# Routing arithmetic of the first half moved from VectorE to GpSimd, with PSUM banks marked as taken

## The chip, the cores and the metric

One core of a Trainium2 chip runs the whole program. The metric is the device time of one execution, in microseconds (us). Five engines work side by side, each through its own queue in order: TensorE (PE, weight loads shown as PEld), VectorE (DVE), ScalarE (ACT), GpSimd (POOL) and SyncE (SP, which here only starts DMAs). Data move between engines through SBUF and through PSUM, the eight accumulator banks that TensorE writes.

## The reference

```python
# attention, q k v: (4, 8, 1152, 64)
q_pool = q.reshape(B, H, S // 2, 2, D).mean(axis=3)
scores = scale * np.matmul(q_pool, k.transpose(0, 1, 3, 2))
scores = scores - np.max(scores, axis=-1, keepdims=True)
attn = np.exp(scores);  attn /= np.sum(attn, axis=-1, keepdims=True) + 1e-09
x = (attn @ v) as 2304 tokens x 512
# mixture of 8 experts, the best two of each token
noisy = x @ w_gate + np.log1p(np.exp(x @ w_noise)) * noise
top2_w = softmax of the two largest of noisy
out[token] += top2_w[k] * (np.maximum(x @ w1[e], 0) @ w2[e])   # for both chosen experts
```

## The kernel before, in words

The program has three stages: attention, routing, experts. Values are held as pairs of 16-bit numbers (a high and a low part), so most products are made of three matmuls.

**Attention** works on 16 pairs (a head of two batches), each with three query groups of 384, 48 segments in all. For each step of work `score` writes a chunk of scores to one of two wide PSUM tiles (`pss`), ScalarE takes the exponential into `pf`, and the low part `pl` = `pf` - high(`pf`) is made by `p_lo` on whichever of POOL (two halves of 128x384, L358) and DVE (one piece of 128x768, L355) the planner chooses. Then `pv` multiplies with the values. Ahead of it run the row maxima: `max_mm` and `max_rest` (L297) on TensorE, `max_relu` on ScalarE, `max_red` (L311) and `rest_red` (L320) on DVE. The four single PSUM banks (`psm`) are shared by the maxima, the `pv` sums and the routing.

**What sets the order.** `Plan` is a list scheduler that runs when the program is written: every piece of work has an engine, a cost, a due key and what it waits for, and the planner writes the pieces into the engines' queues in the order in which its own clock starts them. On the chip each queue runs in that order.

**Routing** is `Route.steps`, a generator that gives one piece at each `yield`. It is run four times: once for the first half of the tokens (`j=0`, nine blocks of 128 tokens, so tiles of 128x72), in the second half of attention; and three times for the second half (`j=1`, three blocks each, 128x24), beginning at the end of attention. These three are called groups 0, 1 and 2 here; what of them the planner has not placed when attention ends is written out by `advance`, in steps of `PACE`, between the pieces of `Moe.early`. A run transposes its rows by DMA into `xTg` tiles (L671; three tiles a group, and four buffers for all of them), multiplies by the gate weights (L681, 36 matmuls a group), evicts (L685), computes a softplus by polynomials (L690 to L734), the noisy logits (L737, L739), the two largest (L744, L748), a one-hot mask (L759), the rank of each token in its expert by matmul (L767, L769), a slot number (L792), a small table beside each row (L796 to L799), and then scatters every row twice into the expert lists `xg` in DRAM (L99, 18 indirect DMAs on POOL's queue for each half).

**Experts.** `Moe.early` works on the first 256 rows of the first two experts, which the first half's scatter has filled, while the second half is routed; `mm1` (L937) and `mm2` (L958) are the matmuls, `flush` evicts `mm1` (L946 on ScalarE, L947 on DVE), `split` (L882, L884) makes the weights' two parts. `Moe.run` loads the other rows (`xT<-xg`, L892) only after the last scatter, and then goes through all experts. `Base.bank` hands out the four `psm` banks in rotation.

Of the kernel before, what the change touches and what calls it, by code (L numbers as in the profile page):

```python
# [9 lines left out]
F32 = mybir.dt.float32  # L10
# [9 lines left out]
P = 128  # L20
# [8 lines left out]
E = 8  # L29
# [37 lines left out]
class Base:  # L67
    def __init__(s, tc, ctx):
        s.tc, s.nc = tc, tc.nc
        s.const = ctx.enter_context(tc.tile_pool(name="const", bufs=1))  # L70
        ps = ctx.enter_context(tc.tile_pool(name="ps", bufs=1, space=PSUM))
        s.wides = [ps.tile([P, 2, 512], F32, name=f"pss{x}") for x in range(2)]
        s.banks = [ps.tile([P, 512], F32, name=f"psm{x}") for x in range(4)]
        s.sp = s.const.tile([1, 1], F32, name="sp")
        s.raw = {"kr": s.const.tile([P, 2 * NK, D], F32, name="kr"), "qr": s.const.tile([P, NCQ, 2, D], F32, name="qr"),
                 "vr": s.const.tile([P, 2 * NK, D], F32, name="vr"), "kn": s.const.tile([P, 2 * NK, P], F16, name="kn")}
        s.given = None
        s.nw = s.nb = 0

    def flat(s, name):  # L80
# [130 lines left out]
class Attn:  # L211
# [306 lines left out]
    def others(s, F0, out):  # L518
# [30 lines left out]
    def route(s, gen, key, deps, slack, soft=False, then=None, pace=0.0):  # L549
        G = s.G  # L550
# [6 lines left out]
        def piece(bank, held):  # L557
# [30 lines left out]
class Route:  # L588
# [55 lines left out]

    def steps(s, j, gs, pool, nt, nu, gap):
        nc = s.nc
        V = nc.vector
        C = 3 * len(gs)

# [7 lines left out]
        def U(shape, dt=F32):  # L657
            n = 1
            for x in shape:
                n *= x  # L660
            t = pool.tile([P, C * 2 * E], dt, name=f"ru{C}", bufs=nu)[:, 0:n]
            if len(shape) == 3:
                return t.rearrange("p (c k e) -> p c k e", c=shape[0], k=shape[1])
            return t.rearrange("p (c e) -> p c e", c=shape[0])
        L = U([C, 2 * E])
        for x, g in enumerate(gs):
# [18 lines left out]
            V.tensor_scalar(L[:, 3 * x:3 * x + 3], ps, 1.0 / (XS * GS), None, op0=ALU.mult)  # L685
            yield (0.0, "SP", 1.35) if gap and x + 1 < len(gs) else None
        lg = L[:, :, 0:E]
        t = L[:, :, E:]
        a = T([C, E])
# [5 lines left out]
        V.tensor_scalar(k, a, LOG2E, RND, op0=ALU.mult, op1=ALU.add)  # L695
        yield
        V.tensor_scalar(k, k, RND, None, op0=ALU.subtract)
        yield
        r = T([C, E])
        V.scalar_tensor_tensor(r, k, -LN2H, a, op0=ALU.mult, op1=ALU.add)  # L700
        yield
        V.scalar_tensor_tensor(r, k, -LN2L, r, op0=ALU.mult, op1=ALU.add)
        kb = T([C, E], I32)
        V.tensor_scalar(kb, k, 127.0, 8388608.0, op0=ALU.add, op1=ALU.mult)
        yield
        p = T([C, E])
        V.tensor_scalar(p, r, EXPC[0], None, op0=ALU.mult)
# [5 lines left out]
        V.scalar_tensor_tensor(e, p, 1.0, kb.bitcast(F32), op0=ALU.add, op1=ALU.mult)  # L713
        yield
        z = T([C, E])
        V.tensor_scalar(z, e, 2.0, None, op0=ALU.add)
        yield
        V.reciprocal(z, z)
        yield
        V.tensor_mul(z, z, e)  # L720
        yield
        z2 = T([C, E])
        V.tensor_mul(z2, z, z)
        yield
        V.tensor_scalar(p, z2, LOGC[0], None, op0=ALU.mult)
        rl = T([C, E])
        V.tensor_scalar(rl, t, 0.0, None, op0=ALU.max)
        yield
        for cc in LOGC[1:]:
            V.scalar_tensor_tensor(p, p, cc, z2, op0=ALU.add, op1=ALU.mult)  # L730
            yield
        V.scalar_tensor_tensor(p, p, 1.0, z, op0=ALU.add, op1=ALU.mult)
        yield
        V.scalar_tensor_tensor(p, p, 2.0, rl, op0=ALU.mult, op1=ALU.add)  # L734
        yield
        c0 = j * NCQ + gs[0] * 3
        V.tensor_mul(p, p, s.nz[:, c0:c0 + C])  # L737
        yield
        V.tensor_add(p, p, lg)  # L739
        yield  # L740
        m8 = T([C, E])
        ix = T([C, E], U32)
        for c in range(C):
            V.max(out=m8[:, c], in_=p[:, c])  # L744
            if c % 3 == 2:
                yield
        for c in range(C):
            V.max_index(out=ix[:, c], in_max=m8[:, c], in_values=p[:, c])  # L748
            if c % 3 == 2:
                yield  # L750
        d = T([C, 1])
# [4 lines left out]
        V.tensor_copy(idx, ix[:, :, 0:2])  # L756
        yield
# [4 lines left out]
        V.memset(mk[:, C], 0.0)  # L762
        yield
        V.tensor_add(mk[:, 0:C], oh[:, :, 0], oh[:, :, 1])
        yield (0.1, "PE", 0.6) if gap else WAIT_RK
        pr = s.B.bank()[:, 0:(C + 1) * E].rearrange("p (c e) -> p c e", e=E)
        nc.tensor.matmul(pr.rearrange("p c e -> p (c e)"), s.tri, mk.rearrange("p c e -> p (c e)"), start=True, stop=False)  # L767
        for c in range(C):
# [3 lines left out]
        sm = T([C, 1])  # L772
        V.tensor_scalar(sm, e2, 1.0, 1e-9, op0=ALU.add, op1=ALU.add)
        yield (0.2, "DVE", 0.35) if gap else None
        rk = U([C + 1, E])
        V.tensor_add(rk, pr, s.n0[:, None, :].to_broadcast([P, C + 1, E]))
        V.reciprocal(w[:, :, 0:1], sm)
        yield
        q = U([C, 2, E])
        V.tensor_mul(q, oh, rk[:, 0:C, None, :].to_broadcast([P, C, 2, E]))  # L780
        s.n0 = s.per.tile([P, E], F32, name=f"n{j}{gs[0]}")
        if j == 0:
            V.tensor_max(s.n0, rk[:, C], s.floor)
# [46 lines left out]
class Moe:  # L830
# [89 lines left out]
    def mm1(s, e, f, a=0, b=CAP):  # L920
# [109 lines left out]
def overflow_body(tc, a, R, w1, w2, out):  # L1030
# [26 lines left out]
    with tc.For_i(0, E, 1) as e:  # L1057
# [15 lines left out]
        with tc.For_i(0, nt, 1):  # L1073
# [102 lines left out]
```

## Time and profile before

| | us |
|---|---|
| median of 3 runs | 889.57 (889.2 to 894.68) |
| the profiled execution | 891.44 |
| its span, first to last instruction | 889.6 |
| PE busy | 812.4 (91%) |
| DVE busy | 532.0 (60%) |
| ACT busy | 444.1 (50%) |
| POOL busy | 393.3 (44%) |

Shares over the whole span mix the stages. Attention lasts to about 442 us, the changeover with the second half's routing to about 503 us, and the rest is the experts. A line such as "L355 DVE TENSOR_TENSOR pl<-pf" is an instruction of line 355 on DVE that writes a tile `pl` from `pf`.

### The profile page before, as it was taken

How to read it: one execution, taken by the hardware profiler on the slowest of the kernel's cores; microseconds unless marked ns; L12 is line 12 of the kernel's file. 1: busy time of each engine (PE TensorE's matmuls, PEld its weight loads, DVE VectorE, ACT ScalarE, POOL GpSimd, SP SyncE). 2: the span in 40 equal slices, each digit the busy share in tenths (PEclk: the TensorE clock that was granted, in tenths of full speed). 3: DMA queues.
4: the chain of work that ended last, by engine and by line, in shares of the span. 5: the costliest groups of instructions: out<-in, count | busy, mean ns of one | idle time of the engine just before them, and what ended most of it. 6: DMA issues, size and time to landing. Idle time of an engine off the chain costs nothing. (4 is left out here: it accounts for less than half of the span.)

```text
span 889.6 us, 21173 instructions
## 1 busy us (share of the span) xinstructions
PE 812.4 (91%) x8686; PEld 534.3 (60%) x8686; DVE 532.0 (60%) x1276; ACT 444.1 (50%) x663; POOL 393.3 (44%) x378
## 2 busy tenths in 40 slices
PE   3889999999989778899979799999999999999995
PEld 1547777677767645678756365756474655647542
DVE  4878898899889898899888141334233231422200
ACT  4658878787877466676534132333233232322310
POOL 4448889887984777674307312020202102020222
PEclk9989999999999889999999999999999999999998
DMA  8899796897899469566568836282927456290143
GB/s 195 174 230 246 159 235 177 194 207 182 196 220 190 117 157 227 122 180 142 126 156 299 203 72 141 74 214 71 226 60 202 84 137 148 72 225 14 24 54 43
DMA packets 213639, 137.81 MB, mean 155 GB/s; under 512 B 150305, under 2 KB 183585, under 8 KB 213537
## 3 DMA queue, kind: packets, MB, share of 16 engines
q1 hardware_dynamic: 204896, 116.33, 53.9%
q0 software_dynamic: 8640, 20.08, 11.1%
q8 instruction: 69, 1.13, 0.5%
q14 instruction: 34, 0.27, 0.1%
HBM read 62.14 MB, written 35.44 MB: 110 GB/s over the span
## 5 line engine op out<-in xcount | busy, mean ns | idle before, releaser
L358 POOL TENSOR_TENSOR pl<-pf 128x384 f16<-128x384 f32 x278 | 269.6, 999 | 103.9 <-ACT pf L350 90.9
L350 ACT ACTIVATE pf<-pss 128x768 f32<-128x768 f32 x216 | 173.5, 813 | 62.6 <-PE pss L343 54.3
L99 POOL DMA_INDIRECT out_dram<-y,mti x40 | 62.2, 1556 | 315.8 <-ACT y L963 306.6
L378 PEld LDWEIGHTS <-pf 128*128 128x128 bf16 x2880 | 158.6, 99 | 47.7 <-issue 18.2
L378 PE MATMUL psm<-vv,pf 128*128 128x65 f16 (+1 forms) x2880 | 168.9, 195 | 2.3 <-DVE mx L311 1.2
L378 PE MATMUL psm<-vv,pl 128*128 128x65 f16 (+1 forms) x1440 | 159.9, 194 | 2.7 <-POOL pl L358 1.9
L342 PE MATMUL pss<-qt,kt 128*128 128x384 f16 (+1 forms) x576 | 151.4, 292 | 2.9 <-ACT pf L350 2.9
L343 PE MATMUL pss<-qt,kt 66*128 66x384 f16 (+1 forms) x576 | 151.7, 292 | 0.1
L947 DVE SCALAR_TENSOR_TENSOR hl<-pss,hh 128x640 f16<-128x640 f32 (+2 forms) x68 | 50.2, 738 | 157.3 <-ACT hh L946 157.3
L378 PEld LDWEIGHTS <-pl 128*128 128x128 f16 x1440 | 127.8, 100 | 3.3 <-POOL pl L358 2.2
L958 PE MATMUL psm<-wh,hh 128*128 128x512 f16 x320 | 122.0, 381 | 0.0
L958 PE MATMUL psm<-wl,hh 128*128 128x512 f16 x320 | 122.0, 381 | 0.0
L958 PE MATMUL psm<-wh,hl 128*128 128x512 f16 x320 | 122.0, 381 | 0.0
L311 DVE CUSTOM_DVE_ANT_0 rd<-psm,rd 128x512 f32<-128x512 f32 x144 | 97.4, 684 | 24.3 <-ACT rd L305 20.1
L946 ACT ACTIVATE hh<-pss 128x640 f16<-128x640 f32 (+2 forms) x68 | 43.2, 635 | 131.6 <-PE pss L937 131.6
L958 PEld LDWEIGHTS <-hh 128*128 128x128 f16 x640 | 62.7, 98 | 74.0 <-issue 0.8
L963 ACT ACTIVATE y<-psm,mg 128x512 f32<-128x512 f32 x40 | 27.5, 688 | 153.9 <-issue 82.1
L297 PE MATMUL psm<-kt,qt 128*128 128x512 f16 (+3 forms) x320 | 79.9, 325 | 23.0 <-DVE mx L311 10.4
L305 ACT ACTIVATE rd<-psm 128x512 f32<-128x512 f32 x144 | 86.1, 598 | 22.4 <-PE psm L297 17.4
L937 PE MATMUL pss<-xT,fh 128*128 128x320 f16 (+1 forms) x448 | 84.4, 305 | 5.7 <-DMA xT<-xg 5.7
L355 DVE TENSOR_TENSOR pl<-pf 128x768 f16<-128x768 f32 x77 | 87.1, 1145 | 0.0
L937 PE MATMUL pss<-xT,wh 128*128 128x320 f16 (+1 forms) x448 | 83.4, 303 | 0.0
(158 smaller groups left out, 1134.7 us busy)
## 6 DMA issues: line engine op xcount, KB each, us to landing
xg<-zt SPq DMA_DIRECT2D x40, 260.0 KB
kr<-in_k_dram SPq DMA_DIRECT2D x32, 288.0 KB
vr<-in_v_dram SPq DMA_DIRECT2D x16, 576.0 KB
kr<-in_moe_w_dram SPq DMA_DIRECT2D x17, 512.0 KB
qr<-in_moe_w_dram SPq DMA_DIRECT2D x16, 512.0 KB
kn<-in_moe_w_dram SPq DMA_DIRECT2D x16, 512.0 KB
qr<-in_q_dram SPq DMA_DIRECT2D x31, 256.0 KB
vr<-in_moe_w_dram SPq DMA_DIRECT2D x15, 512.0 KB
```

Of the source, the lines that this page charges most:

```text
L99: i = nc.gpsimd.indirect_dma_start(out=out, out_offset=bass.IndirectOffsetOnAxis(ap=idx, axis=0), in_=src, in_offset=None, **kw)
L297: s.nc.tensor.matmul(ps[r, o:o + m.shape[1] * P], s.G.buf["qt", i][:, c, r], m, start=True, stop=True)
L305: s.nc.scalar.activation(s.G.buf["rd", i, c], s.G.buf["D", i, c], AF.Relu)
L311: s.nc.vector.tensor_tensor_reduce(out=rd, in0=s.G.buf["S", i, c], in1=rd, scale=1.0, scalar=-3.0e38, op0=ALU.add, op1=ALU.max, accum_out= ...
L342: mm(ps[:, a, o:o + w], kt[:, hh * NK + kc, :], qf[:, q0:q0 + w], start=True, stop=False)
L343: mm(ps[:, a, o:o + w], kt2[0:66, hh * NK + kc, :], qf2[0:66, q0:q0 + w], start=False, stop=True)
L350: s.nc.scalar.activation(s.parts(u)[0], s.G.buf["ps", u][:, :, 0:SG], AF.Exp, scale=0.125 / (IN_SCALE * IN_SCALE))
L355: s.nc.vector.tensor_sub(pl, pf, ph)
L358: s.nc.gpsimd.tensor_sub(pl[:, a], pf[:, a], ph[:, a])
L378: mm(o[:, 0:x], src[:, t % 2, ci * P:ci * P + P], vv[:, hh * NK + kc, a:a + x], start=st, stop=last and src is pl, skip_group_check=True)
L937: nc.tensor.matmul(ps[:, i, 0:N], w[:, dc, f * P:(f + 1) * P], xT[:, 2 * dc + x, i * N:(i + 1) * N], start=(n == 0), stop=(n == 11))
L958: nc.tensor.matmul(ps, h[:, f, b * P:(b + 1) * P], w[:, f, :], start=(n == 0), stop=(n == 23))
```

## The change

In the first half's routing (`steps(0, ...)`) the elementwise steps go to POOL. A DVE instruction that does two operations on two tensors (`scalar_tensor_tensor`) becomes two on POOL: a `tensor_scalar` into a scratch tile `tm`, and a `tensor_tensor`; the planner sees two pieces. Reciprocals, MAX8, the index search, the one-hot compare, the reduction and what reads PSUM stay on DVE. The first step takes max(-t, t), so the signs of the steps behind it change. The planner is told that those pieces are POOL's (`home`). Apart from this, `bank` now skips a bank that has been handed out and whose reader has not been written yet. The second half's routing stays on DVE; only one multiplication in it (L789) comes one place later.

```diff
     def bank(s):
+        s.taken = None
         if s.given is not None:
             return s.given
         s.nb += 1
-        return s.banks[s.nb % 4]
+        assert len(s.busy) < 4
+        while s.nb % 4 in s.busy:
+            s.nb += 1
+        s.taken = s.nb % 4
+        s.busy.add(s.taken)
+        return s.banks[s.taken]
...
-        s.route(R.steps(0, (0, 1, 2), s.sm, 14, 6, 0.8), 245, [s.ev[n] for n in range(24)], 3.0, then=then, pace=0.8)
+        s.route(R.steps(0, (0, 1, 2), s.sm, 14, 6, 0.8, "POOL"), 245, [s.ev[n] for n in range(24)], 3.0, then=then, pace=0.8, home="POOL")
...
-            wait, eng, cost = d if isinstance(d, tuple) else (0.0, "DVE", 0.3)
+            wait, eng, cost = d if isinstance(d, tuple) else (0.0, home, 0.3)
...
+        W = V if eng == "DVE" else nc.gpsimd
+        dve = None if eng == "DVE" else (0.1, "DVE", 0.3)
...
+        def stt(o, x, c, y, op0, op1):
+            if W is V:
+                V.scalar_tensor_tensor(o, x, c, y, op0=op0, op1=op1)
+                return
+            W.tensor_scalar(tm, x, c, None, op0=op0)
+            yield
+            W.tensor_tensor(o, tm, y, op=op1)
...
-        V.scalar_tensor_tensor(a, t, -1.0, t, op0=ALU.mult, op1=ALU.min)
-        yield
-        V.tensor_scalar(a, a, -87.0, None, op0=ALU.max)
+        V.scalar_tensor_tensor(a, t, -1.0, t, op0=ALU.mult, op1=ALU.max)
+        yield
+        W.tensor_scalar(a, a, 87.0, None, op0=ALU.min)
...
-            V.scalar_tensor_tensor(p, p, cc, r, op0=ALU.add, op1=ALU.mult)
+            yield from stt(p, p, cc, r, ALU.add, ALU.mult)
...
-            V.tensor_copy(mt[:, :, 0:1], s.tok[:, c0 + 3 * x:c0 + 3 * x + 3, None])
+            W.tensor_copy(mt[:, :, 0:1], s.tok[:, c0 + 3 * x:c0 + 3 * x + 3, None])
...
             s.nc.scalar.activation(hh, ps, AF.Relu)
             s.nc.vector.scalar_tensor_tensor(hl, ps, 0.0, hh, op0=ALU.max, op1=ALU.subtract)
+            s.B.busy.discard(bk)
```

Since the planner's clock runs differently once these pieces stand elsewhere, everything behind them is ordered anew. Three places follow; line numbers of the second of each pair are those of the changed file.

GpSimd's queue from the place where the first half's arithmetic begins, before:

```order
L358 TENSOR_TENSOR pl_114<-pf_113 128x384 x2
L358 TENSOR_TENSOR pl_110<-pf_109 128x384 x2
L358 TENSOR_TENSOR pl_112<-pf_111 128x384 x2
L358 TENSOR_TENSOR pl_114<-pf_113 128x384 x2
L358 TENSOR_TENSOR pl_116<-pf_115 128x384 x2
L358 TENSOR_TENSOR pl_118<-pf_117 128x384 x2
```

and now (`rt` and `ru` are the routing's tiles):

```order
L365 TENSOR_TENSOR pl_114<-pf_113 128x384 x2
L365 TENSOR_TENSOR pl_110<-pf_109 128x384 x2
L712 TENSOR_SCALAR rt_5344<-rt_5344 128x72
L715 TENSOR_SCALAR rt_5361<-rt_5344 128x72
L717 TENSOR_SCALAR rt_5361<-rt_5361 128x72
L679 TENSOR_SCALAR rt_5345<-rt_5361 128x72
L681 TENSOR_TENSOR rt_5385<-rt_5345,rt_5344 128x72
```

Twenty-four such steps stand there, then one `pl` pair, then twenty-two more; the next four chunks of `pl` on either side of that pair have gone to DVE's queue. DVE holds 87 `pl` pieces in all, before 77; POOL 129 pairs, before 139.

SyncE's queue, the transposes for groups 0, 1 and 2 (their rows are `xr_83`, `xr_84`, `xr_85`), with the semaphores that each waits for, before:

```order
L671 DMA_TRANSPOSE xTg<-xr_83 128x8x128 [waits DMAHW6_49,DVE_49]
L671 DMA_TRANSPOSE xTg<-xr_83 128x8x128 [waits DMAHW7_49]
L671 DMA_TRANSPOSE xTg<-xr_83 128x8x128 [waits DMAHW0_49]
L671 DMA_TRANSPOSE xTg<-xr_84 128x8x128 [waits DMAHW1_49,DVE_49]
L671 DMA_TRANSPOSE xTg<-xr_84 128x8x128 [waits DMAHW6_49,DMAHW2_49,PE_49]
L671 DMA_TRANSPOSE xTg<-xr_84 128x8x128 [waits DMAHW7_49,DMAHW3_49,PE_49]
L671 DMA_TRANSPOSE xTg<-xr_85 128x8x128 [waits DMAHW0_49,DMAHW4_49,DVE_49,PE_49]
L671 DMA_TRANSPOSE xTg<-xr_85 128x8x128 [waits DMAHW5_49,DMAHW1_49,PE_49]
L671 DMA_TRANSPOSE xTg<-xr_85 128x8x128 [waits DMAHW2_49,PE_49]
```

and now:

```order
L689 DMA_TRANSPOSE xTg<-xr_83 128x8x128 [waits DMAHW6_49,DVE_49]
L689 DMA_TRANSPOSE xTg<-xr_83 128x8x128 [waits DMAHW7_49]
L689 DMA_TRANSPOSE xTg<-xr_84 128x8x128 [waits DMAHW0_49,DVE_49]
L689 DMA_TRANSPOSE xTg<-xr_85 128x8x128 [waits DMAHW1_49,DVE_49]
L689 DMA_TRANSPOSE xTg<-xr_84 128x8x128 [waits DMAHW6_49,DMAHW2_49,PE_49]
L689 DMA_TRANSPOSE xTg<-xr_83 128x8x128 [waits DMAHW7_49,DMAHW3_49,PE_49]
L689 DMA_TRANSPOSE xTg<-xr_85 128x8x128 [waits DMAHW4_49,DMAHW3_49,PE_49]
L689 DMA_TRANSPOSE xTg<-xr_84 128x8x128 [waits DMAHW5_49,DMAHW0_49,PE_49]
L689 DMA_TRANSPOSE xTg<-xr_85 128x8x128 [waits DMAHW2_49,PE_49]
```

The groups, one after the other before, are now mixed, and group 0's third tile is sixth. From the fifth on each transposes into a buffer that TensorE must have read: the fifth waits for the matmuls on the first tile, the sixth for those on the second, and so on.

DVE's queue at the evictions of the three groups' gate products (L685 before, L704 now; `hl` belongs to `mm1`), before:

```order
L685 TENSOR_SCALAR ru_8131<-psm_67 128x48
L710 SCALAR_TENSOR_TENSOR rt_8315<-rt_8315,rt_8310 128x24
L690 SCALAR_TENSOR_TENSOR rt_8374<-ru_8131 128x24
...
L718 RECIPROCAL rt_8397<-rt_8397 128x24
L700 SCALAR_TENSOR_TENSOR rt_8437<-rt_8395,rt_8374 128x24
L720 TENSOR_TENSOR rt_8397<-rt_8397,rt_8393 128x24
L685 TENSOR_SCALAR ru_8211<-psm_65 128x48
```

and now:

```order
L971 SCALAR_TENSOR_TENSOR hl<-pss_63,hh 128x256
L704 TENSOR_SCALAR ru_8150<-psm_66 128x48
L710 SCALAR_TENSOR_TENSOR rt_8378<-ru_8150 128x24
L712 TENSOR_SCALAR rt_8378<-rt_8378 128x24
L704 TENSOR_SCALAR ru_8194<-psm_67 128x48
L715 TENSOR_SCALAR rt_8418<-rt_8378 128x24
L710 SCALAR_TENSOR_TENSOR rt_8420<-ru_8194 128x24
L704 TENSOR_SCALAR ru_8213<-psm_66 128x48
```

Before, group 0 was past its reciprocal when group 2's eviction came, 27 rows behind its own; now the three evictions stand within seven rows, and the groups go on in step.

## Rows read from the trace of the kernel before

**Rows 1.** Busy us by engine in stretches, granted clock (PEclk), DMA share

```profile
300.00:316.00 16.00, 12.22 (x176) 9.01 (x176) 12.70 (x56) 6.57 (x12) 11.49 (x14) 0.79 0.15 36
316.00:332.00 16.00, 11.08 (x82) 6.00 (x82) 15.37 (x55) 8.93 (x17) 10.34 (x12) 0.79 0.64 162
443.60:469.30 25.70, 19.86 (x219) 14.05 (x217) 20.71 (x140) 9.00 (x16) 0.03 (x1) 0.91 0.63 163
497.10:503.10 6.00, 0.32 (x3) 0.05 (x1) 0.00 (x0) 0.69 (x1) 0.04 (x1) 0.93 0.66 139
503.10:889.60 386.50, 375.54 (x2208) 216.31 (x2207) 111.05 (x178) 111.77 (x148) 62.37 (x41) 0.99 0.47 110
```

**Rows 2.** Whom TensorE waited for, 284 to 332 us: total, times, longest

```profile
PE psm L297 <- DVE mx L311: 5.5, 4, 4.7
PE psm L297 <- DVE mx L320: 1.9, 1, 1.9
```

**Rows 3.** DVE in order of time, first half's routing: start, us, instruction

```profile
289.26 0.71 DVE L692 TENSOR_SCALAR rt<-rt 128x72 f32<-128x72 f32 x1
290.01 0.20 DVE L695 TENSOR_SCALAR rt<-rt 128x72 f32<-128x72 f32 x1
...
298.42 3.90 DVE L730 SCALAR_TENSOR_TENSOR rt<-rt,rt 128x72 f32<-128x72 f32 x5
302.24 0.68 DVE L311 CUSTOM_DVE_ANT_0 rd<-psm,rd 128x512 f32<-128x512 f32 x1
```

**Rows 4.** DVE's groups, 284 to 443.6 us: count, busy us, mean ns

```profile
L355 DVE TENSOR_TENSOR pl<-pf 128x768 f16<-128x768 f32 x40 | 45.1, 1150 | 0.0
```

**Rows 5.** POOL's groups in the same stretch

```profile
L358 POOL TENSOR_TENSOR pl<-pf 128x384 f16<-128x384 f32 x83 | 78.2, 968 | 51.8 <-ACT pf L350 46.6 <-PE psm L378 3.0 <-PE pss L343 1.9
...
L842 POOL IOTA tro<- 128x5 f32 x1 | 0.2, 179 | 0.6 <-POOL pl L358 0.6
```

**Rows 6.** The chain of waits at the changeover: start, us, what

```profile
445.82 0.89 PE psm L681 x36
446.71 1.33 PE psm L937 x12
...
452.30 4.03 DMA xTg<-xr
...
456.38 0.47 PE psm L681 x12
456.87 0.21 DVE ru L685
```

**Rows 7.** SyncE in order of time

```profile
414.67 3.18 SPq L640 DMA_TRANSPOSE xe<-xg  x1
...
427.45 0.37 SPq L816 DMA_DIRECT2D kr<-in_moe_w_dram  x1
437.40 16.16 SPq L671 DMA_TRANSPOSE xTg<-xr  x9
```

**Rows 8.** The tile xTg's transposes: ns shortest/median/longest, first and last start

```profile
L671 SPq DMA_TRANSPOSE xTg<-xr x9: 1231/1258/2258, 437.4 to 452.3; - x9
```

**Rows 9.** DVE in order of time, up to group 0's release

```profile
465.52 1.16 DVE L884 SCALAR_TENSOR_TENSOR wl<-qr,wh 128x1024 f16<-128x1024 f32 x1
...
466.69 0.18 DVE L764 TENSOR_TENSOR ru<-ru 128x24 f16<-128x24 f32 x1
466.78 0.18 DVE L720 TENSOR_TENSOR rt<-rt,rt 128x24 f32<-128x24 f32 x1
...
468.93 0.07 DVE L799 MEMSET xr<- 128x9 f32 x1
```

**Rows 10.** POOL in order of time: the fifth-last pl pair, first and last scatter

```profile
413.93 2.48 POOL L358 TENSOR_TENSOR pl<-pf 128x384 f16<-128x384 f32 x2 [2.54 <-ACT pf L350]
...
469.27 0.99 POOL L99 DMA_INDIRECT xg<-xr,rt  x1 [27.07 <-DVE rt L739]
...
494.90 0.97 POOL L99 DMA_INDIRECT xg<-xr,rt  x1 [0.31 <-issue]
```

More of the change, by code (lines that the diff above doesn't have):

```diff
@@ L76, in __init__ @@
                  "vr": s.const.tile([P, 2 * NK, D], F32, name="vr"), "kn": s.const.tile([P, 2 * NK, P], F16, name="kn")}
-        s.given = None
+        s.given = s.taken = None
         s.nw = s.nb = 0
+        s.busy = set()
     def flat(s, name):
@@ L544, in then, with route @@
                 op("SP", 2.6, 400 + 4 * e, lambda e=e: R.early(e), ready=G.now + 20.0)
-        s.route(R.steps(0, (0, 1, 2), s.sm, 14, 6, 0.8), 245, [s.ev[n] for n in range(24)], 3.0, then=then, pace=0.8)
+        s.route(R.steps(0, (0, 1, 2), s.sm, 14, 6, 0.8, "POOL"), 245, [s.ev[n] for n in range(24)], 3.0, then=then, pace=0.8, home="POOL")
         for g in range(3):
             s.route(R.steps(1, (g,), R.rp, 36, 15, 0.3), 450 + 9 * g, [s.ev[24 + 3 * i + g] for i in range(NH)], 0.7, True)
-    def route(s, gen, key, deps, slack, soft=False, then=None, pace=0.0):
+    def route(s, gen, key, deps, slack, soft=False, then=None, pace=0.0, home="DVE"):
         G = s.G
@@ L643, in early, with steps @@
         s.pre[e] = x, mt
-    def steps(s, j, gs, pool, nt, nu, gap):
+    def steps(s, j, gs, pool, nt, nu, gap, eng="DVE"):
         nc = s.nc
         V = nc.vector
+        W = V if eng == "DVE" else nc.gpsimd
+        dve = None if eng == "DVE" else (0.1, "DVE", 0.3)
         C = 3 * len(gs)
@@ L685, in steps @@
             V.tensor_scalar(L[:, 3 * x:3 * x + 3], ps, 1.0 / (XS * GS), None, op0=ALU.mult)
-            yield (0.0, "SP", 1.35) if gap and x + 1 < len(gs) else None
+            s.B.busy.discard(bk)
+            yield (0.0, "SP", 1.35) if gap and x + 1 < len(gs) else dve
         lg = L[:, :, 0:E]
         t = L[:, :, E:]
-        a = T([C, E])
-        V.scalar_tensor_tensor(a, t, -1.0, t, op0=ALU.mult, op1=ALU.min)
+        a, tm = T([C, E]), None if W is V else T([C, E])
+        V.scalar_tensor_tensor(a, t, -1.0, t, op0=ALU.mult, op1=ALU.max)
@@ L691, in steps @@
         yield
-        V.tensor_scalar(a, a, -87.0, None, op0=ALU.max)
+        W.tensor_scalar(a, a, 87.0, None, op0=ALU.min)
         yield
         k = T([C, E])
-        V.tensor_scalar(k, a, LOG2E, RND, op0=ALU.mult, op1=ALU.add)
+        W.tensor_scalar(k, a, -LOG2E, RND, op0=ALU.mult, op1=ALU.add)
         yield
-        V.tensor_scalar(k, k, RND, None, op0=ALU.subtract)
+        W.tensor_scalar(k, k, RND, None, op0=ALU.subtract)
         yield
         r = T([C, E])
-        V.scalar_tensor_tensor(r, k, -LN2H, a, op0=ALU.mult, op1=ALU.add)
+        yield from stt(r, k, -LN2H, a, ALU.mult, ALU.subtract)
@@ L701, in steps @@
         yield
-        V.scalar_tensor_tensor(r, k, -LN2L, r, op0=ALU.mult, op1=ALU.add)
+        yield from stt(r, k, -LN2L, r, ALU.mult, ALU.add)
         kb = T([C, E], I32)
-        V.tensor_scalar(kb, k, 127.0, 8388608.0, op0=ALU.add, op1=ALU.mult)
+        W.tensor_scalar(kb, k, 127.0, 8388608.0, op0=ALU.add, op1=ALU.mult)
         yield
         p = T([C, E])
-        V.tensor_scalar(p, r, EXPC[0], None, op0=ALU.mult)
+        W.tensor_scalar(p, r, EXPC[0], None, op0=ALU.mult)
         yield
@@ L709, in steps @@
         for cc in EXPC[1:]:
-            V.scalar_tensor_tensor(p, p, cc, r, op0=ALU.add, op1=ALU.mult)
+            yield from stt(p, p, cc, r, ALU.add, ALU.mult)
             yield
         e = T([C, E])
-        V.scalar_tensor_tensor(e, p, 1.0, kb.bitcast(F32), op0=ALU.add, op1=ALU.mult)
+        yield from stt(e, p, 1.0, kb.bitcast(F32), ALU.add, ALU.mult)
         yield
         z = T([C, E])
-        V.tensor_scalar(z, e, 2.0, None, op0=ALU.add)
-        yield
+        W.tensor_scalar(z, e, 2.0, None, op0=ALU.add)
@@ L718, in steps @@
+        yield dve
         V.reciprocal(z, z)
         yield
-        V.tensor_mul(z, z, e)
+        W.tensor_mul(z, z, e)
         yield
         z2 = T([C, E])
-        V.tensor_mul(z2, z, z)
+        W.tensor_mul(z2, z, z)
         yield
-        V.tensor_scalar(p, z2, LOGC[0], None, op0=ALU.mult)
+        W.tensor_scalar(p, z2, LOGC[0], None, op0=ALU.mult)
         rl = T([C, E])
-        V.tensor_scalar(rl, t, 0.0, None, op0=ALU.max)
+        W.tensor_scalar(rl, t, 0.0, None, op0=ALU.max)
@@ L728, in steps @@
         yield
         for cc in LOGC[1:]:
-            V.scalar_tensor_tensor(p, p, cc, z2, op0=ALU.add, op1=ALU.mult)
+            yield from stt(p, p, cc, z2, ALU.add, ALU.mult)
             yield
-        V.scalar_tensor_tensor(p, p, 1.0, z, op0=ALU.add, op1=ALU.mult)
+        yield from stt(p, p, 1.0, z, ALU.add, ALU.mult)
         yield
-        V.scalar_tensor_tensor(p, p, 2.0, rl, op0=ALU.mult, op1=ALU.add)
+        yield from stt(p, p, 2.0, rl, ALU.mult, ALU.add)
         yield
         c0 = j * NCQ + gs[0] * 3
-        V.tensor_mul(p, p, s.nz[:, c0:c0 + C])
+        W.tensor_mul(p, p, s.nz[:, c0:c0 + C])
@@ L738, in steps @@
         yield
-        V.tensor_add(p, p, lg)
-        yield
+        W.tensor_add(p, p, lg)
+        yield dve
         m8 = T([C, E])
@@ L745, in steps @@
             if c % 3 == 2:
-                yield
+                yield dve
         for c in range(C):
@@ L749, in steps @@
             if c % 3 == 2:
-                yield
+                yield dve
         d = T([C, 1])
@@ L756, in steps @@
         V.tensor_copy(idx, ix[:, :, 0:2])
-        yield
+        yield dve
         oh = U([C, 2, E])
@@ L776, in steps @@
         V.tensor_add(rk, pr, s.n0[:, None, :].to_broadcast([P, C + 1, E]))
+        s.B.busy.discard(bk)
         V.reciprocal(w[:, :, 0:1], sm)
@@ L784, in steps @@
         else:
-            V.tensor_copy(s.n0, rk[:, C])
-        yield
+            W.tensor_copy(s.n0, rk[:, C])
+        yield dve
         rs = T([C, 2])
         V.tensor_reduce(rs, q, axis=AX.X, op=ALU.add)
-        V.tensor_mul(w[:, :, 1:2], w[:, :, 0:1], e2)
-        yield
+        yield dve
         sl = T([C, 2], I32)
         V.scalar_tensor_tensor(sl, idx, float(FULL), rs, op0=ALU.mult, op1=ALU.add)
+        yield
+        W.tensor_mul(w[:, :, 1:2], w[:, :, 0:1], e2)
         for x, g in enumerate(gs):
@@ L929, in mm1 @@
         else:
-            ps = s.B.wide()
+            ps, s.B.taken = s.B.wide(), None
+        bk = s.B.taken
         m = 1 if b - a <= 512 else 2
@@ L940, in mm1 @@
         v = lambda t: t[:, f, a:b].rearrange("p (a n) -> p a n", a=m)
-        s.late.append((v(hh), v(hl), ps[:, 0:m, 0:N]))
+        s.late.append((v(hh), v(hl), ps[:, 0:m, 0:N], bk))
     def flush(s, keep=0):
         while len(s.late) > keep:
-            hh, hl, ps = s.late.pop(0)
+            hh, hl, ps, bk = s.late.pop(0)
             s.nc.scalar.activation(hh, ps, AF.Relu)
             s.nc.vector.scalar_tensor_tensor(hl, ps, 0.0, hh, op0=ALU.max, op1=ALU.subtract)
+            s.B.busy.discard(bk)
     def mm2(s, e, b):
@@ L954, in mm2 @@
         ps = s.B.bank()
+        bk = s.B.taken
         n = 0
@@ L963, in mm2 @@
         nc.scalar.activation(y, ps, AF.Copy, scale=g)
+        s.B.busy.discard(bk)
         s.rows.append((ti, y, e))
@@ L1090, in overflow_body @@
             for f in range(8):
+                R.B.busy.clear()
                 ps = R.B.bank()[:, 0:P]
@@ L1099, in overflow_body @@
                 V.scalar_tensor_tensor(hl[:, f], ps, 0.0, hh[:, f], op0=ALU.max, op1=ALU.subtract)
+            R.B.busy.clear()
             ps = R.B.bank()
```

16 lines of the change are left out of this document (9 added, 7 removed).

## The prediction, made before the changed kernel ran

> **What bounds the kernel now.** I read the busy time by stretches first, since shares of the whole span mix three stages. From 503.1 us on TensorE is busy for 375.5 of 386.5 us at a granted clock of 0.99 [rows 1]: nothing of this change lies there, and that stage simply starts earlier or later. Just before it TensorE does nothing for 6 us (0.32 busy) [rows 1]; in those it waits for the experts' rows, which are loaded only after the second half's 18 scatters. So the start of the last stage is set by the last scatter. Read back along the chain of waits, the scatters start at 469.27 us, when the DVE has finished group 0's table (468.93) [rows 9, 10], and group 0's arithmetic hangs in DVE's queue behind the eviction of group 2 at 456.87, which hangs on a transpose by DMA that took 4.03 us to arrive [rows 6]. In attention the stretch with the first half's routing, 284 to 332 us, is the poor one: from 300 to 332 TensorE is busy 23.3 of 32 us at a clock of 0.79, DVE 28.1 [rows 1]. The waits name DVE: 7.4 us for the row maxima L311 and L320 [rows 2], which stood in the queue behind a solid run of routing steps from 289.26 to 302.24 us [rows 3]. So two places count: DVE's load in attention, and the path from attention's end to the last scatter.
>
> **The first half's arithmetic.** Removed from DVE: the run from 289.26 to 302.24, 13.0 us [rows 3], less one reciprocal that stays (0.6), so 12.4; and 22 later small steps, 0.20 each by the undisturbed row at 290.01 [rows 3], so 4.4. Together 16.8 us. Added to DVE: the planner moves ten chunks of `pl` from POOL to it (87 against 77), 1.15 each [rows 4], so 11.5. Net 5.3 us less on DVE. On POOL ten pairs go, 2 x 0.968 x 10 = 19.4 us [rows 5], and 63 small steps come: 24 and 22 in two runs around one `pl` pair, and 17 later. No 128x72 step on POOL is in the trace. Below stands an instruction with 5 columns, 0.179 us; above the half of `pl` with 384 columns, 0.968 [rows 5]. Between them by columns, 0.18 + 0.79 x 67/379 = 0.32 us; I take 0.33, nearer the lower row because 72 columns are. The 46 steps of the two runs then take 15 us and the pair 1.9. What covers them: between the two hand-overs DVE has 43 instructions of its own, eight of them `pl` at 1.15 (9.2) and 35 others at 0.28 (15.37 us by 55 [rows 1]) to 0.44; so 19 to 25 us. POOL is done first while a step stays under about 0.48 us.
>
> Since TensorE's waits there end on DVE, attention should end earlier by what DVE saves, 5.3 us, plus a little of the slow clock: I take 6. From below: nothing, if the planner's new order wastes it. From above: all of the 7.4 us of waits, and what the slow clock cost, 23.3 x 0.21 = 4.9; together 12.
>
> One contention is in the rows themselves: the same 128x72 shape took 0.71 us at 289.26 and 0.20 at 290.01 [rows 3], the long ones while POOL worked on `pl`. After the change POOL's short steps meet DVE's long `pl`. The Trainium skill, SBUF — State Buffer, section "SBUF: two separate sides", says that DVE and GpSimd share a port pair as an exclusive lock for a whole instruction, and that the other fully blocks. The two lengths agree with it; by that rule a POOL step may stand behind a whole `pl` of DVE, which is the second rival below, where the sum by rows alone has no such term.
>
> **The DMAs that are moved.** The first half's scatters come later in POOL's queue: five `pl` pairs follow the last one, eight did. The fifth-last pair starts at 413.93 [rows 10], so the last scatter lies at about 412 instead of 399. The loads of the early rows (`xe`) need it, and are moved in SyncE's queue behind the weight load of 427.45 [rows 7]. Two of them with their small tables take some 7.3 us (3.18 for the first), so they end by about 435; SyncE was idle until 437.40, and TensorE needs the first at 442. I cost this at nothing; the cover is 2 us, and a longer delay would show as a wait of the first L937 for `xe`.
>
> **The changeover.** The order of the second half's routing changes though its arithmetic does not. Before, TensorE does 36 matmuls of `mm1`, group 0's 36, then 36 and group 1's, 12 and group 2's; now 72, groups 0 and 1 together, 12, group 2. Step by step, from attention's end as before: 12 `mm1` matmuls take 1.33 us [rows 6], so TensorE reaches group 0 not at 445.8 but 4.0 later, 449.8. It reads two tiles (12 matmuls each, 0.3). Only then do the fifth and sixth transposes start, 1.26 each on SyncE [rows 8], and the sixth is group 0's third tile: started at 451.4. From start to use the last transpose before took 4.03 [rows 6], of which 1.26 is its own time on the queue; I take 3, since fewer loads run beside it. TensorE gets it at 454.4 and ends group 0 at 454.7. That releases the seventh, and the eighth, group 1's third tile, starts at 456.0 and is there at 459.0. Twelve `mm1` matmuls follow (1.3), the ninth transpose lands at about 460.6, and group 2 is done at about 461.3 instead of 456.85: **4.5 us later** (2 us at 2.0 a landing, 6.3 at 4.03).
>
> DVE takes the three evictions within seven rows, so all that follows waits for group 2. From there to group 0's last table row DVE took 12.06 us (456.87 to 468.93 [rows 6, 9]). Now there are 45 more small steps before that place, 0.09 from start to start when three groups alternate (466.69 to 466.78 [rows 9]), so 4.05; two more L884 of 1.16 [rows 9], 2.3; and two more triples of MAX8 and index search, 18 instructions, 1.6. So **7.9 us more** (6 to 9). The first scatter moves by 12.4 us. The 18 scatters then run as before, 25.6 us from first to last [rows 10], perhaps a little faster as DVE has less to do beside them: I take **12 us** for the changeover (8 to 15). TensorE's early experts, which also slip, end before the scatters and cost nothing. Marking banks removes one wait of a `mm1` for a bank (about 1 us, under the same cover) and adds no instruction.
>
> **Sum.** -6 + 12 = +6 us. The profiled execution, 891.44 us with a span of 889.6, is 1.9 above the median of 889.57; I put the difference on the median: 889.57 + 6 = **895.6 us**.
>
> **The rivals.**
>
> The forecast, slower by 6 us, I give 0.5; its own range is 888 to 903.
>
> First rival, faster: attention gets back everything it loses between 284 and 332 us, 12 us, and the transposes land quickly, so that the changeover costs only 8. It decides from the point where attention's gain passes the changeover's cost. For it: the waits end on DVE alone [rows 2], and the maxima now stand ahead of what replaces the routing. Against: DVE saves only 5.3 us. 889.6 - 12 + 8 = 885.6 us; 0.17.
>
> Second rival, POOL becomes the bound: its steps wait behind DVE's long instructions. From 0.48 us a step POOL is late, and with it `pl`, TensorE and the maxima. At 0.7 us, between the two bounds, the 46 steps are 46 x 0.22 = 10 us late, and the gain of 6 turns into a loss of 4: 889.6 + 4 + 12 = 905.6 us. For it: the long rows of the same shape [rows 3], and that every step waits for the one before. Against: POOL's pairs, also shared with DVE, average 0.968 for five times the columns. 0.25.
>
> Third rival: the mixed order costs nothing, as TensorE has 6 idle us there anyway [rows 1] and the scatters' pace and not their start sets the end. Then 889.6 - 6 = 883.6. Against: POOL stood idle for 27 us before the first scatter [rows 10]. 0.08. That the change does nothing is excluded by the queues, which differ.
>
> **How the numbers follow.** About 1% (8.9 us) is what a measurement here can tell from no change, so faster means under 880.7 and slower over 898.5. The forecast puts 0.27 of its half above 898.5; the second rival 0.75 of its 0.25; together 0.32. Faster comes from the ends of the first and third rivals, 0.05. The rest, 0.63, is the same. The range 885 to 906 holds the forecast's own range, most of the second rival and the upper part of the first.
>
> **What would show it.** DVE busy in attention down by about 5 us; no run of routing steps ahead of L311 near 300 us, and TensorE's waits there under 3 us; POOL's 128x72 steps at 0.25 to 0.45 us from start to start (over 0.5: the second rival). L681 waiting for `xTg` twice, 3 to 4 us each; the three evictions within 8 us and the last about 20 us ahead of the first scatter; the first scatter about 6 us later than 469. Wrong altogether if the first scatter comes no later than 465 or the last stage does not follow the last scatter.

## The result, and the profile after

The changed kernel took 902.49 us (median, 901.66 to 903.43) where the kernel before took 890.56 in the runs beside it: a ratio of 1.0112, 95% interval [1.0076, 1.0149], so 10 us (7 to 13) slower; the medians alone lie 11.9 us apart, which is inside that interval. The profiled executions agree: spans of 899.6 and 889.6 us. The forecast was +6; the time lies within the range of 885 to 906, in the class "slower by over 1%", to which 0.32 had been given.

Line numbers of the changed kernel are higher: L311 is now L318, L320 L327, L671 L689, L681 L700, L685 L704, L937 L961, L99 L106, L355 and L358 L362 and L365.

Read in the same order as before, by stretches (columns as in [rows 1]; the changed kernel's first, cut where its changeover has its milestones):

```profile
300.00:316.00 16.00, 11.77 (x180) 8.51 (x179) 9.90 (x21) 7.79 (x13) 13.94 (x28) 0.89 0.43 132
316.00:332.00 16.00, 11.06 (x164) 8.20 (x161) 10.39 (x53) 9.06 (x15) 15.45 (x23) 1.00 0.34 82
448.80:463.00 14.20, 5.96 (x125) 4.99 (x122) 1.68 (x11) 0.77 (x2) 0.00 (x0) 0.64 0.72 179
463.00:481.30 18.30, 12.34 (x65) 5.82 (x64) 18.20 (x169) 5.36 (x9) 0.00 (x1) 0.84 0.30 107
504.28:512.21 7.93, 0.00 (x1) 0.00 (x0) 0.00 (x0) 0.45 (x1) 0.96 (x1) 0.62 0.65 169
512.20:899.60 387.40, 376.38 (x2208) 216.61 (x2207) 110.66 (x178) 111.70 (x148) 62.50 (x41) 0.98 0.47 110
```

and the stretch of the kernel before that answers to its third line, from group 0's gate matmuls to the last eviction:

```profile
445.80:456.90 11.10, 8.28 (x157) 7.48 (x154) 8.26 (x34) 3.74 (x8) 0.00 (x0) 1.00 0.84 167
```

Two things are to be seen. In attention TensorE is busy for 22.8 of the 32 us of [rows 1], where it was 23.3. Its granted clock is now 0.89 and then 1.00, where it was 0.79, so more work fits into these us (344 matmul records, 258 before), but TensorE still stands idle as long. DVE fell from 28.1 to 20.3: DVE is no longer busy, and POOL is (29.4). And at the changeover TensorE is busy for 6 of 14.2 us at a granted clock of 0.64, where it had 8.3 of 11.1 at full clock.

The difference of 10.0 us, from milestone to milestone of the two traces:

| | before | after | difference |
|---|---|---|---|
| attention ends | 441.9 | 440.5 | -1.4 |
| from there to the last group's eviction | 15.0 | 22.3 | +7.3 |
| from there to the first scatter | 12.4 | 18.5 | +6.1 |
| first to last scatter | 25.63 | 22.98 | -2.65 |
| last scatter to TensorE's next matmul | 8.15 | 7.93 | -0.2 |
| from there to the end | 386.55 | 387.4 | +0.85 |

**Attention.** Whom TensorE waited for, 284 to 332 us, changed kernel (as [rows 2]), and then whom DVE waited for, 284 to 345 us:

```profile
PE psm L304 <- DVE mx L327: 5.1, 2, 4.2
PE psm L304 <- DVE qn L336: 2.6, 1, 2.6
PE psm L304 <- DVE mx L318: 1.5, 1, 1.5
```

```profile
DVE rt L738 <- POOL rt L736: 4.8, 1, 4.8
DVE rt L764 <- POOL rt L759: 3.3, 1, 3.3
DVE rt L799 <- POOL rt L794: 2.3, 1, 2.3
```

TensorE still waits for the row maxima and for what is made of them (qn), 9.2 us in all. They no longer stand behind routing arithmetic; most of the 9.2 us stands behind a DVE instruction that waits for POOL. The reciprocal L738 held DVE's queue for 4.8 us, and the maximum L327 is the next row behind it. The reason is in POOL's rows (start, us, instruction), and in DVE's beside them:

```profile
293.60 0.39 POOL L679 TENSOR_SCALAR rt<-rt 128x72 f32<-128x72 f32 x1
294.07 0.34 POOL L681 TENSOR_TENSOR rt<-rt,rt 128x72 f32<-128x72 f32 x1
294.49 0.84 POOL L724 TENSOR_SCALAR rt<-rt 128x72 int32<-128x72 f32 x1
...
295.88 1.08 POOL L679 TENSOR_SCALAR rt<-rt 128x72 f32<-128x72 f32 x1
...
303.27 0.39 POOL L736 TENSOR_SCALAR rt<-rt 128x72 f32<-128x72 f32 x1
303.62 1.61 POOL L365 TENSOR_TENSOR pl<-pf 128x384 f16<-128x384 f32 x2
```

```profile
293.50 0.68 DVE L318 CUSTOM_DVE_ANT_0 rd<-psm,rd 128x512 f32<-128x512 f32 x1
...
294.11 1.11 DVE L362 TENSOR_TENSOR pl<-pf 128x768 f16<-128x768 f32 x1
...
295.75 1.86 DVE L362 TENSOR_TENSOR pl<-pf 128x768 f16<-128x768 f32 x2
...
303.69 0.60 DVE L738 RECIPROCAL rt<-rt 128x72 f32<-128x72 f32 x1 [4.79 <-POOL rt L736]
304.21 0.49 DVE L327 TENSOR_REDUCE mx<-psm 128x3 f32<-128x384 f32 x1
```

Undisturbed, a step lasts 0.34 or 0.39 us and the next, which waits for it, starts 0.08 later: 0.45 from start to start. Eleven of the 46 last 0.7 to 1.1 us, each beside a `pl` or an L288 of DVE. Together 24 steps took 13.6 us and 22 took 12.9: 0.57 and 0.59 a step, where 0.33 was forecast and 0.3 stands in the planner.

**Changeover.** The chain of waits, as [rows 6], without its pieces of 0.05 us and less:

```profile
448.83 0.60 PE psm L700 x24
449.43 0.95 SPq L689
450.48 3.13 DMA xTg<-xr
453.66 1.14 PE psm L700 x36
454.80 0.61 SPq L689
455.51 3.23 DMA xTg<-xr
458.79 0.49 PE psm L700 x12
459.28 2.57 PE psm L961 x12
461.85 0.91 PE psm L700 x36
462.79 0.21 DVE ru L704
```

It is the forecast ladder: two tiles read, the sixth transpose, group 0, the eighth, group 1, twelve matmuls, group 2. The two scatters that answer to [rows 10], and the loads of the early rows that answer to [rows 7]:

```profile
481.30 0.98 POOL L106 DMA_INDIRECT xg<-xr,rt  x1 [40.54 <-DVE ru L802]
...
504.28 0.96 POOL L106 DMA_INDIRECT xg<-xr,rt  x1 [0.31 <-issue]
```

```profile
426.45 3.10 SPq L647 DMA_TRANSPOSE xe<-xg  x1
429.59 0.58 SPq L649 DMA_DIRECT2D mte<-xg  x1
430.21 2.55 SPq L647 DMA_TRANSPOSE xe<-xg  x1
```

### The profile page after: what moved, and what is told of

Its sections match the earlier page's. It is cut to its first block, busy times and chain, and to the rows that moved or that the text cites. A ratio compares the mean times of both kernels' runs of the same rounds, so it can differ in the third digit from the quotient of the medians.

```text
span 899.6 us, 21166 instructions
## 1 busy us (share of the span) xinstructions
PE 810.0 (90%) x8686; PEld 533.0 (59%) x8686; DVE 524.8 (58%) x1240; ACT 442.6 (49%) x663; POOL 401.8 (45%) x421
## 4 chain that ended last, share of the span: by engine, by line
PE 43%; DVE 2%; POOL 2%; DMA 2%; issue 1%; SPq 0%; ACT 0%; POOLq 0%; ACTq 0%; DVEq 0%
PE pss L961 21%; PE psm L984 20%; POOL xg L106 2%; PE psm L961 1%; DMA xTg<-xr 1%; DMA xT<-xg 1%; DVE rt L677 1%; DVE wl L907 0%; PE psm L700 0%; POOL out_dram L106 0%; DMA xg<-xr,rt 0%; SPq L689 0%; DVE rt L768 0%; DVE hl L971 0%; ACT y L989 0%
## 5 line engine op out<-in xcount | busy, mean ns | idle before, releaser
L365 POOL TENSOR_TENSOR pl<-pf 128x384 f16<-128x384 f32 x258 | 252.3, 1007 | 89.1 <-ACT pf L357 73.8
L106 POOL DMA_INDIRECT out_dram<-y,mti x40 | 62.3, 1558 | 316.5 <-ACT y L989 310.9
L318 DVE CUSTOM_DVE_ANT_0 rd<-psm,rd 128x512 f32<-128x512 f32 x144 | 97.1, 682 | 20.3 <-ACT rd L312 18.2
L362 DVE TENSOR_TENSOR pl<-pf 128x768 f16<-128x768 f32 x87 | 98.0, 1138 | 0.0
L961 PE MATMUL pss<-xT,fh 128*128 128x320 f16 (+1 forms) x448 | 85.0, 307 | 8.2 <-DMA xT<-xg 8.2
L961 PE MATMUL pss<-xT,wh 128*128 128x320 f16 (+1 forms) x448 | 83.4, 303 | 0.0
```

Source lines behind the costliest of these rows:

```text
L106: i = nc.gpsimd.indirect_dma_start(out=out, out_offset=bass.IndirectOffsetOnAxis(ap=idx, axis=0), in_=src, in_offset=None, **kw)
L318: s.nc.vector.tensor_tensor_reduce(out=rd, in0=s.G.buf["S", i, c], in1=rd, scale=1.0, scalar=-3.0e38, op0=ALU.add, op1=ALU.max, accum_out= ...
L362: s.nc.vector.tensor_sub(pl, pf, ph)
L365: s.nc.gpsimd.tensor_sub(pl[:, a], pf[:, a], ph[:, a])
L961: nc.tensor.matmul(ps[:, i, 0:N], w[:, dc, f * P:(f + 1) * P], xT[:, 2 * dc + x, i * N:(i + 1) * N], start=(n == 0), stop=(n == 11))
```

## The experiments

Each was timed against the kernel before on the same chip, whose medians there were 893 to 894 us. The same instructions ended attention up to 3 us apart from one profiled execution to the next (441.9 in the kernel before, 444.8 in e2), so totals are compared by ratio, and inside traces times are counted from attention's end.

**e1 to e3: the order of the groups.** e1 is the changed kernel with the groups set back to where they stood before, when attention ends (`R.second` holds their three generators, `R.tr` counts the transposes queued):

```diff
-            gens = A.run(F0, out)
+            A.run(F0, out)
+            for g, n in ((0, 3), (1, 2)):       # group, transposes
+                while R.tr.get(g, 0) < n:
+                    next(R.second[g])
+            gens = [[t, g, PACE] for t, g in zip((2.24, 0.0, 0.38), R.second)]
```

> The changed kernel with one thing put back: the second half's three groups start the changeover in the state in which they stood before the change (three transposes of group 0 and two of group 1 queued, group 2 a little behind), so that they run one after the other; the first half's routing stays on GpSimd. Theory A (the loss is the mixed order at the changeover, attention itself gained 1.4 us): first scatter at about 468 us (469.3 less 1.4), last one near 493, total 1 to 3 us under the kernel before, about 888. Theory B (the loss comes with GpSimd's routing itself, for example the early rows that come later): it stays at about 902. Between them, 893 to 898, the groups' order is half of it.

e2 is the converse, in the kernel before: `ready=406.0` for the groups' first piece, `((0, 2),)` and `(0.59, 0.0, 0.38)` in the lines above. That kernel does not mark banks, so in the mixed order two pieces can share one, and part of the values is overwritten; e6 below is the same order with the banks marked.

> The kernel before, routing on VectorE, with nothing but the second half's groups held back so that they start the changeover in the state of the changed kernel (two transposes of group 0 queued, groups 1 and 2 not begun) and mix as they do there. Theory A: attention ends as before at 441.9 us, first scatter at about 482.5 (13 us later), scatters then 4 us shorter, total about 10 us over the kernel before, 900. Theory B: the kernel before's time, 889.6, within 2 us.

e3 adds to e1 a delay after a group's eviction:

```diff
-            yield (0.0, "SP", 1.35) if gap and x + 1 < len(gs) else dve
+            yield (0.0, "SP", 1.35) if gap and x + 1 < len(gs) else ((3.4, 0.9, 0.0)[g], "DVE", 0.3) if j else dve
```

> As e1, transposes and gate matmuls of the three groups one after the other, but groups 0 and 1 held after their evictions, so that the three groups' arithmetic goes in step on VectorE as in the changed kernel. It parts the changeover's loss into its two terms. By the changed kernel's trace, late transposes are 7.3 us of it (last eviction at 462.8 against 456.9, attention ending 1.4 earlier) and the arithmetic in step 6.1 (18.5 against 12.4 us from there to the first scatter). Theory A: last eviction at about 455.5, first scatter at about 474, total 6 over e1, some 894. If the transposes are all of it: as e1. If the arithmetic is all of it: as the changed kernel, 902.

Measured: e1 0.9977 [0.9952, 1.0003], e2 1.0113 [1.0067, 1.0158], e3 1.0045 [1.0025, 1.0066]. So the order alone takes 12 us from the changed kernel and gives 10 to the old one, wherever the first half is computed: theory A. The first scatter of e1 came at 471.4 and not at 468, since attention ended later in that execution (443.1). The scatters of e2 take 23.9 us from first to last, 1.8 less than before and not 4. e3, with late arithmetic and punctual transposes, lies 6 us over e1 (0.0068 x 893) and 6 under the changed kernel. So the arithmetic in step costs 6 us by itself, and about as much is left for the late transposes, which no run has alone. In e3's trace:

```profile
440.15 0.40 PE psm L385 x7
...
455.82 0.21 DVE ru L707
```

```profile
475.38 0.98 POOL L106 DMA_INDIRECT xg<-xr,rt  x1 [34.53 <-DVE ru L800]
```

The last eviction is 15.3 us after attention's end, as before; the first scatter 19.6 behind it, as after.

**e5, e6: the marking of banks.** e5 leaves the first half on DVE (`s.route(R.steps(0, (0, 1, 2), s.sm, 14, 6, 0.8), ...)`, no `home`); e6 mixes its groups as e2 did.

> The changed kernel with the first half's routing left on VectorE: the marking of banks alone (and the new sign of three steps). The planner then leaves the second half's groups as in the kernel before, three transposes of group 0 and two of group 1 queued. Theory A: the marking costs and gives nothing by itself, within 2 us of the kernel before. Rival: skipping taken banks makes matmuls wait for other banks, or takes waits away: over 4 us either way.

> As e5, and the second half's groups held back so that they mix as in the changed kernel: what e2 did, now with the banks marked (in e2 two pieces could be handed one bank, so part of its values was overwritten, while instructions and sizes were the same). Theory A: 10 us over e5, and the first scatter 13 us later behind attention's end than in e5; whether the routing's first half is on GpSimd does not matter to it. Rival: e2's 10 us came from shared banks; then within 4 us of e5.

Measured: e5 0.9990 [0.9971, 1.0010], e6 1.0121 [1.0082, 1.0161]. The marking is free, and e6 is 11.7 us over e5 (0.0131 x 894): e2's loss was not one of shared banks. Counted where the program is written, `bank` skips no bank in e5, and one bank, once, in e6 and in the changed kernel, during the mixed groups: the marking is what the mixed order needs. From attention's end, all of these traces fall into three kinds:

| | to the last eviction | from it to the first scatter |
|---|---|---|
| one after the other: before, e5, e1, e4 | 15.0, 16.5, 15.7, 14.9 | 12.4, 12.6, 12.6, 12.2 |
| in step, transposes in order: e3 | 15.3 | 19.6 |
| mixed: after, e2, e6 | 22.3, 21.9, 22.4 | 18.5, 18.4, 18.8 |

**e8: why some steps are long.** In `p_lo`, for chunks 138 to 155:

```diff
-            s.nc.vector.tensor_sub(pl, pf, ph)
+            for a in (slice(0, 1), slice(1, 2)) if 138 <= u < 156 else (slice(0, 2),):
+                s.nc.vector.tensor_sub(pl[:, a], pf[:, a], ph[:, a])
```

> The changed kernel, same order everywhere, with eight of VectorE's pieces of pl beside the two runs of GpSimd steps written as two halves of 128x384 (0.5 us each instead of 0.95). It asks what makes ten of the 46 steps 0.7 to 1.1 us long while the others take 0.34 to 0.39. Theory (a step stands still while one VectorE instruction of pl runs): no step beside the halves over 0.75 us, more steps of 0.5 to 0.75. Rival (GpSimd and VectorE share bandwidth evenly over the time): steps beside the halves stay at 0.7 to 1.1 as with the whole piece. The total may change by 2 us.

POOL's rows, and DVE's beside them, in part:

```profile
293.73 0.91 POOL L680 TENSOR_SCALAR rt<-rt 128x72 f32<-128x72 f32 x1
294.72 0.36 POOL L682 TENSOR_TENSOR rt<-rt,rt 128x72 f32<-128x72 f32 x1
295.17 0.57 POOL L680 TENSOR_SCALAR rt<-rt 128x72 f32<-128x72 f32 x1
```

```profile
293.62 0.75 DVE L288 SCALAR_TENSOR_TENSOR kn<-kr,kn 128x576 f16<-128x576 f32 x1
294.29 1.21 DVE L363 TENSOR_TENSOR pl<-pf 128x384 f16<-128x384 f32 x2
```

Beside the halves no step is over 0.65 us and ten are of 0.50 to 0.65; the three that stay over 0.7 stand beside L288, which was left whole. The runs fell to 0.52 us a step. So a step stands still for one DVE instruction and not for a share of the time. This is what the Trainium skill says (SBUF — State Buffer, "SBUF: two separate sides"): the port pair is locked for a whole instruction. The section names as DVE's side of it instructions in a two-port mode or with two inputs in SBUF, and the trace agrees: `pl` has two, while the row maximum L318 reads one of its two from PSUM and lasts 0.68 us; in the changed kernel's trace none of the six steps that run beside it is over 0.39 us (293.60 above is one). The kernel's one run, 901.7 us, is within the noise of the changed kernel's.

**e4, e7, e9: what the planner is told.** e4 is e1 with 0.55 for 0.3, e7 the changed kernel with 0.65 and nothing else:

```diff
-            wait, eng, cost = d if isinstance(d, tuple) else (0.0, home, 0.3)
+            wait, eng, cost = d if isinstance(d, tuple) else (0.0, home, 0.65 if home == "POOL" else 0.3)
```

> As e1, and the planner is told 0.55 us instead of 0.3 for each step of the first half's routing on GpSimd (0.57 was measured from start to start in the two runs of steps). Theory A: VectorE's waits of 4.8, 3.3 and 2.3 us for GpSimd, behind which the row maxima stand, came from the wrong price; told the right one the planner puts those VectorE pieces later, the three waits fall under 1 us each, and attention ends 2 to 5 us earlier than in e1, total 883 to 886. Rival: GpSimd's chain is 5 us longer than its place whatever the planner thinks; then later work waits for it instead and it is e1 within 2 us, or slower as the second half's groups must wait less.

> The changed kernel with one number changed: the planner is told 0.65 us for each step of the first half's routing on GpSimd instead of 0.3. By its own clock the planner then ends with group 0's three transposes and two of group 1's queued, so the groups go one after the other without help, and it places VectorE's pieces that wait for GpSimd later than at 0.55. Theory A: as e4 or better, 881 to 887 where the kernel before has 890; VectorE's waits for GpSimd under 2 us each. Rival (price only shifts the wait to TensorE's pv, which needs GpSimd's pl): as the kernel before, within 2 us.

Measured: e4 0.9934 [0.9911, 0.9958], e7 0.9920 [0.9890, 0.9951]; 6 and 7 us faster than before. e4 differs from e1 in the price alone, which is worth 4 us there (0.0043 x 893). e7 lies 17 us under the changed kernel, but some 12 of these, by e1, belong to the groups, which its planner puts one after the other again. DVE's three waits for POOL, 10.4 us in the changed kernel, are 6.1 in e4 (2.5, 1.8 and 1.8, not under 1 each as expected) and 1.2 in e7:

```profile
DVE rt L738 <- POOL rt L736: 1.0, 1, 1.0
...
DVE rt L764 <- POOL rt L759: 0.2, 1, 0.2
```

and the stretch that bounded attention is full, at full clock:

```profile
300.00:316.00 16.00, 14.56 (x230) 10.84 (x227) 14.79 (x31) 11.58 (x20) 13.41 (x24) 1.00 0.62 155
316.00:332.00 16.00, 14.83 (x265) 11.43 (x263) 15.60 (x60) 11.51 (x18) 15.17 (x22) 1.00 0.39 92
```

e7's attention ends 13 us earlier than that of the kernel before, but 5.5 of them were lost at once. Its chain of waits, in part:

```profile
431.00 0.47 PE psm L700 x12
...
431.83 5.09 DMA xe<-xg
...
436.96 2.72 PE pss L961 x12
```

The early rows' load stood on SyncE behind five transposes. e9 takes that away:

```diff
-                op("SP", 2.6, 400 + 4 * e, lambda e=e: R.early(e), ready=G.now + 20.0)
+                op("SP", 2.6, 400 + 4 * e, lambda e=e: R.early(e), ready=G.now + 6.0)
```

> As e7 with one more number changed: the loads of the early rows (xe) may be queued 6 us after the planner's last scatter of the first half instead of 20, so on SyncE they stand ahead of the second half's transposes. In e7's trace attention ended 13 us earlier than before, but the first expert matmuls waited until 437.0 for xe, whose load stood behind five transposes and started at 431.8; TensorE stood still for 5.5 us. Theory A: with xe there in time the changeover starts at once, the first scatter comes 3 to 5 us earlier than in e7 and the total is 3 to 5 us under e7, some 10 to 12 us under the kernel before. Rival (the second half's last transposes and VectorE's arithmetic set the first and last scatter anyway, or xe now waits on SyncE for the scatters and delays the weights): e7 within 2 us.

Measured: 0.9865 [0.9832, 0.9899], 12 us faster than the kernel before and 5 under e7 by the ratios (0.0055 x 894). In its trace `xe` is loaded from 407.9 on, TensorE goes from attention to the experts without a gap, and the last scatter comes 11 us earlier than before and 4.7 earlier than in e7; the first comes at 459.8, only 1.6 us earlier than in e7, where 3 to 5 were expected:

```profile
428.49 0.39 PE psm L385 x7
428.88 1.31 PE pss L961 x12
```

```profile
483.75 0.96 POOL L106 DMA_INDIRECT xg<-xr,rt  x1 [0.30 <-issue]
```

## Why the prediction was right, and where it was not

- **The sign and its place: right.** The changeover decides, and it costs 11.4 us by the table (7.3 + 6.1 - 2.65 - 0.2 + 0.85) for a forecast of 12. e1, e2, e5 and e6 show that the groups' order is the cause.
- **Its terms: each mis-sized, and partly against each other; that 12 came out so nearly is luck.** Late transposes were put at 4.5 us and measured 7.3. The landings were right (3.1 and 3.2 for 3); what was missing is TensorE's clock: with 8.2 us of waiting in that stretch it was granted 0.64 (1.00 before), and the twelve `mm1` matmuls took 2.57 us for the 1.33 of [rows 6]. The rest lies in up to 0.5 us at each rung of the ladder. The arithmetic in step was put at 7.9 and measured 6.1; the forecast added its steps to 12 us in which DVE, before, also stood idle for 1.4 (busy 11.0 of 12.4), and in step it was never idle (18.2 of 18.3 above). The gain in the scatters was put at 0.4 and measured 2.65. Not foreseen: 0.85 us in the last stage, which TensorE entered after some 8 us of idling and went through at a granted clock of 0.98, not 0.99.
- **Attention: the step that failed.** The text took 0.33 us for a POOL step, by columns between [rows 5]; it is 0.57 to 0.59, over the 0.48 named as the point from which POOL is late. Two parts were left out: 0.08 between a step and the one that waits for it, and the long steps beside DVE, which [rows 3] had shown the other way round. So the second rival happened in a small size: 46 x 0.1 = 4.6 us late, and DVE waited 4.8 at the first hand-over and 3.3 at the second.

  The 0.48 was itself too kind. It sets 46 steps against all that DVE has between the two hand-overs at the ends and leaves out the `pl` pair of 1.9 us among them; but the first 24 steps are awaited on their own, by the reciprocal. For them DVE had work until 298.9 (303.69 less the wait of 4.79), 8.9 us from the first step on, which is 0.37 a step: there even the undisturbed 0.45 comes late.

  By the count of its exponentials attention was 4.5 us ahead at 335 us and gave 3 back, while DVE (46.3 of 48 us busy from 332 to 380) and POOL (40.4) were nearly full; that this is why is read from the busy times and not tested. It came to -1.4 instead of -6. One pair of executions does not show a gain so small, but e1 and e3 have the same attention as the changed kernel and agree: from the 79th exponential on, at about 179 us, to the last the changed kernel, e1 and e3 took 2.0, 2.3 and 1.9 us less than the kernel before, while e2, e5 and e6, with the arithmetic on DVE, took 4.0 and 1.1 more and 0.7 less. So there is a gain of some 2 to 3 us, but not of 6.

  The pace of POOL and the place of the hand-over in DVE's queue both enter: in e8, at 0.52 us a step and in the same order, the two waits fell to 3.0 and 0.6 us. But e4 and e7 show that the place decides: in e7 the chain on POOL is slower still (0.65 and 0.67 us a step) and DVE has 89 `pl` pieces for 87, but the maximum L327 stands at 299.67, ahead of the reciprocal at 306.27, and e7 won 13 us. What else the new price moved was not taken apart.
- **Right as well:** the early rows cost nothing (the second load starts at 430.2, none takes over 6.7 us to land, and TensorE goes on to them at 440.3 without a wait); DVE's load from 284 us to attention's end fell by 5.5 us, 141.6 to 136.1 (5.3 forecast). **Wrong:** TensorE's waits of under 3 us there (9.2).
- **The chances.** 0.63 lay on "the same", as the forecast stood 3 us below the bound; the measured ratio lies just above it.

## What to carry to other kernels

When a generated order decides, look at what a local change does to the order far behind it: here 12 us came from three groups that had come to start within 0.6 us of each other on the planner's clock. Work that is moved to a slower engine needs its measured price in the planner, taken from start to start in a dependent chain beside the neighbour's real load; one wrong number turned a gain of 13 us in attention into 1.4. The 0.65 that served was above the 0.57 to 0.59 of the first trace, but near what e7's own shows. And a stage that ends earlier only helps if the loads that the next stage needs are queued earlier too.

## What had not been expected of the hardware

A dependent chain of 128x72 steps on POOL runs at 0.45 us a step by itself and at 0.57 to 0.59 beside DVE's `pl` (0.65 to 0.67 in e7, where DVE is busier). In the changed changeover (448.8 to 463.0 us), where TensorE stood in two waits for transposes, its granted clock was 0.64; in the stretch of the kernel before that answers to it, 1.00. The same stretch had 0.64 and 0.68 in e2 and e6, with 8.2 us of such waits in either, and 0.93 and 0.96 in e1 and e3, with 2.9 and 2.5. Its two levels are 1.2 and 2.4 GHz, so it spent most of that stretch at the lower one, and twelve matmuls there took 2.57 us, about twice the 1.33 of [rows 6].
